# Low parts of differences and of the last weights on GpSimd, one tile's splits issued later, and a product cut in two around the mixing products

## The chip, the core and the metric

The kernel runs on one core of one Trainium2 chip. Its engines are TensorE (PE, with PEld for its weight loads), VectorE (DVE), ScalarE (ACT), GpSimd (POOL) and SyncE (SP), which issues most of the transfers. The metric is the device time of one execution in microseconds; the time before is the median of three runs.

## The reference, cut to what matters

An attention over a narrow local window with a few global columns (8 heads of 64, 768 positions, batch 2), then two blocks. All inputs are 32-bit floats.

```python
def _moe_ref(x, U, V, w_ch1, w_ch2):            # x: 2 x 768 x 512
    xt = x.transpose(0, 2, 1)
    h = xt @ U @ V                              # mixing over positions, rank 32
    u = x + h.transpose(0, 2, 1)
    ch = np.maximum(u @ w_ch1, 0.0) @ w_ch2     # 512 -> 2048 -> 512
    return u + ch

def _moe2_ref(x, mu_k, mu_r, w_k, w_v, w_r):
    x_prev = np.concatenate([np.zeros((B, 1, D), dtype=np.float32), x[:, :-1, :]], axis=1)
    xk = mu_k * x + (1.0 - mu_k) * x_prev
    xr = mu_r * x + (1.0 - mu_r) * x_prev
    k = np.maximum(xk @ w_k, 0.0)               # 512 -> 1024
    v = k * k @ w_v                             # 1024 -> 512
    r = 1.0 / (1.0 + np.exp(-(xr @ w_r)))
    return r * v
```

## The kernel before, in words

**Split numbers.** Each matrix is held as two parts: a high part (a rounded copy, made by ScalarE) and a low part (what the copy left out, a subtraction). A product of two such matrices is three matmuls (`PASS`): high x high, high x low, low x high. The subtraction of a low part has both operands in SBUF and can run on DVE or on POOL. The weights arrive as 64-bit floats and are converted (`conv_steps`): `cvt` (L655, DVE), `c1` (L660, ACT), `c2` (L664, DVE), `c3` (L668, DVE), `high` (L672, ACT), `low` (L676, POOL unless told DVE). A weight is queued with `queue_weight` on a list `bgq`, and `bg` takes one entry of 128 x 512 from it: its load through SP into one of three buffers `stg`, and its steps.

**Stages.** The state is `yp`, 512 rows of features in four blocks of 128 by 2 x 769 columns. It is worked on in three column chunks of 512 (`chunk`: c = 0 lies in batch 0, c = 1 half in each, c = 2 in batch 1). First come the attention and, woven into it, the first block's mixing for batch 0 and the first channel product; the order of each engine there is written out by a planner of the kernel itself (`Flow`, with costs by kind of step). After that the code emits steps in an order made by `weave`, which merges lists evenly, and the framework's scheduler may start a later step before an earlier one whose inputs or buffers are not ready.

**The part after the planner.** The mixing for batch 1 (`u_steps(1)`): transposes, `gms`, `gs`, and then for each feature block the product `hps` (L856) and its addition to `yp` (L861), first for 256 columns, then for 512. `u_split` makes the high and low part of the result for the channel products (L899, L901). Channel products: `ch1` (L926, 512 -> 512 of the 2048 columns, results by L930 and L934) and `ch2` (L948, four of them for each chunk and quarter, one for each output block, each of 12 matmuls into one bank of PSUM, emptied by the addition L952). PSUM banks are of two kinds, `a` and `t`, four of each; `hps` and the products of L948 (`bps`) take `t`.

**The pair product.** For the last three quarters of the 2048 columns, chunks 1 and 2 are multiplied together (`st_pair`) with seven products of half size (L1019) in place of eight. For that `diff_raw` computes differences of the chunks (L972) into `raws`, a tile of the pool of `slot_b`, and `diff_split` calls `parts`, which makes their high (L991) and low part (L992), three for each of two row tiles k. `diff_late` does the same for the fourth (L996, L997). The sums of weights that the pair product needs are made in L730 to L733 and split in L739 and L740.

**The end.** The weights wr, wk and wv of the second block are queued during the last quarter. `st_mix` makes xr and xk (L1204 to L1208), `m_r` is L1241, `m_k` L1221 with its low part on POOL (L1231), `m_out` L1256, L1259 and the store.

Of the kernel before, what the change touches and what calls it, by code (L numbers as in the profile page):

```python
# [7 lines left out]
F32 = mybir.dt.float32  # L8
# [201 lines left out]
def body(tc, out, q, k, v, lim, UV, w1, w2, mu_kr, wk, wv, wr):  # L210
    nc = tc.nc
    with ExitStack() as ctx:
# [403 lines left out]
        def path(general):  # L616
            if general:
                attention_general()
            with ExitStack() as pctx, ExitStack() as fence:
# [6 lines left out]
                def bank(tag, nm):  # L626
                    return pp_.tile([128, 512], F32, tag=tag, name=nm, bufs=banks[tag])
# [69 lines left out]
                def queue_weight(name, src, kt, n, sl):  # L697
                    view = [s.rearrange("p (l k n) -> p l k n", l=2, n=n) for s in sl]
                    per = kt // len(sl)
                    wt[name] = (view, per)  # L700
                    for c0 in range(0, n, 512):
                        for kk in range(kt):
                            hi = view[kk // per][:, 0, kk % per, c0:c0 + 512]
                            lo = view[kk // per][:, 1, kk % per, c0:c0 + 512]
                            s = src[kk * 128:(kk + 1) * 128, c0:c0 + 512]
                            steps = conv_steps((128, 512), hi, lo)
                            if name in ("wr", "wk", "wv") and kk % 2:
                                steps[-1] = ("lo", lambda z, f=steps[-1][1]: f(z, "DVE"))
                            bgq.append((lambda d, s=s: nc.sync.dma_start(out=d, in_=s), steps))

                def wsl(name, l, kk, c0, n):
                    view, per = wt[name]
                    return view[kk // per][:, l, kk % per, c0:c0 + n]
# [193 lines left out]
                def chunk(buf, kk, c, shift=0):  # L907
                    if c == 0:
                        return [(0, 512, buf[:, kk, 1 - shift:513 - shift])]
                    if c == 2:  # L910
                        return [(0, 512, buf[:, kk, 1026 - shift:1538 - shift])]
                    return [(0, 256, buf[:, kk, 513 - shift:769 - shift]),
                            (256, 512, buf[:, kk, 770 - shift:1026 - shift])]
# [23 lines left out]
                def m_ch1(g, c, f, mk=None):  # L937
                    ch1_mm(g, c, f, mk)
                    ch1_high(g, c, f)
                    ch1_low(g, c, f)  # L940

                def m_ch2(g, c, o):
                    r = rs[g, c]
                    ps = bank("t", "bps")
                    n = 0
                    for f in range(4):
                        for lw, lx in PASS:
                            nc.tensor.matmul(ps, lhsT=wsl(("w2", g), lw, f, o * 128, 128), rhs=r[:, lx, f, :],  # L948
                                             start=(n == 0), stop=(n == 11))
                            n += 1  # L950
                    for a, e, ys in chunk(yp, o, c):
                        nc.vector.tensor_tensor(out=ys, in0=ps[:, a:e], in1=ys, op=ALU.add)  # L952

                diffs, sums = [], {}

# [28 lines left out]
                def diff_split(k):  # L984
                    return [lambda x=x, t=t: parts(diffs[0], x, k, raws[4 * k + t]) for x, t in enumerate((0, 1, 3))]
# [3 lines left out]
                def parts(d, x, k, raw):  # L989
                    h, o = d[:, 0, x, k, :], d[:, 1, x, k, :]  # L990
                    nc.scalar.copy(out=h, in_=raw)  # L991
                    nc.vector.tensor_tensor(out=o, in0=raw, in1=h.bitcast(F32), op=ALU.subtract)  # L992

                def diff_late(k):
                    h, o = us[2][:, 0, k, :], us[2][:, 1, k, :]
# [73 lines left out]
                def weave(*streams):  # L1069
                    items = []  # L1070
                    for n, s in enumerate(streams):
                        items += [((x + 0.5) / len(s), n, x, f) for x, f in enumerate(s)]
                    for *_, f in sorted(items, key=lambda v: v[:3]):
                        f()

                def st_ch1(g, c, mk):
                    return [lambda f=f: m_ch1(g, c, f, mk) for f in range(4)]

                def st_ch2(g, c):
                    return [lambda o=o: m_ch2(g, c, o) for o in range(4)]  # L1080
# [4 lines left out]
                def st_bg(n):  # L1085
                    return [lambda: bg(1)] * n
# [93 lines left out]
                    u_split(1, kk, slot_d, 0)  # L1180
                weave(u1[6:8], c0[:1])
                weave(c0[1:3])
                for kk in range(4):
                    u1[8 + kk]()
                    u_split(1, kk, slot_d, 1)
                weave(c0[3:])
                weave(u1[12:])
                actx.close()
                open_slots("sc")
# [77 lines left out]
                def st_diff(*ks_):  # L1267
                    return [f for k in ks_ for f in diff_raw(k)]

                diff_tiles()  # L1270
                weave(st_ch1(0, 1, slot_c), [lambda kk=kk: u_split(2, kk, slot_d) for kk in range(4)] + st_diff(0))
                weave(st_ch1(0, 2, slot_c), st_diff(1) + diff_split(0) + diff_split(1))
                late_ = [lambda k=k: diff_late(k) for k in range(2)]
                if G0 == 1:
                    queue_pair(1)
                else:
                    queue_g(1, slot_a, None)
                weave(st_ch2(0, 1), late_ + st_bg(2))
                queue_g(1, None, slot_c)
                weave(st_ch2(0, 2), st_bg(2))  # L1280
                for g in range(1, NG):
# [53 lines left out]
```

## Time and profile before

| | |
|---|---|
| time, median of 3 runs | 511.78 us (511.73 to 514.96) |
| the profiled execution: time / span | 512.37 us / 510.6 us |
| PE busy / DVE / ACT / POOL | 495.5 / 351.3 / 248.4 / 166.8 us |
| granted TensorE clock | 0.999 |
| moved by DMA, over the span | 91 GB/s from and to HBM |

The profile is one execution. The span is the time from its first to its last instruction; the execution's time as measured from outside is 1.77 us longer. A busy PE is not PE at its peak: matmuls overlap, and the end of each is modelled. An idle time of an engine is put down to what ended last before it.

### The profile page before, as it was taken

To read this page: it belongs to the slowest core of one execution; us is meant where nothing else is said; L and a number is where in the kernel's file an instruction comes from. 1 tells how busy PE (TensorE), PEld (TensorE's weight loads), DVE (VectorE), ACT (ScalarE), POOL (GpSimd) and SP (SyncE) were. 2 spreads that over 40 slices of the span, in tenths; PEclk is the share of its full clock that TensorE was granted. 3 is DMA by queue.
4 is the path that set the end of the run, shared out by engine and by line. 5 is a ranking of instruction groups with operands and counts; after the bars stand their busy time and mean duration, and the time that the engine had idled before them with its cause. 6 is when DMAs were issued, how large, how long until landed. Compare 5 with 4: busy or idle time off the path is not lost.

```text
span 510.6 us, 8677 instructions
## 1 busy us (share of the span) xinstructions
PE 495.5 (97%) x3278; PEld 403.5 (79%) x3278; DVE 351.3 (69%) x756; ACT 248.4 (49%) x566; POOL 166.8 (33%) x217
## 2 busy tenths in 40 slices
PE   7899999999999999999999999999999999999995
PEld 4677688778877888888888887888888888888885
DVE  7899988999998879558794599999055057301211
ACT  6999986554432533025330275736883167013400
POOL 7767685020560534005440033122530034002400
PEclk9999999999999999999999999999999999999999
DMA  8888733310334023300242025333001000100011
GB/s 325 295 310 293 238 113 121 122 42 1 124 101 148 0 83 120 127 1 13 81 155 83 0 64 155 113 107 99 0 21 42 21 1 0 56 28 1 0 44 46
DMA packets 13586, 47.18 MB, mean 92 GB/s; under 512 B 1760, under 2 KB 2144, under 8 KB 13536
## 3 DMA queue, kind: packets, MB, share of 16 engines
q1 hardware_dynamic: 13248, 46.28, 27.0%
q8 instruction: 28, 0.46, 0.4%
q10 hardware_dynamic: 288, 0.26, 0.2%
q14 instruction: 22, 0.18, 0.1%
HBM read 43.39 MB, written 3.15 MB: 91 GB/s over the span
## 4 chain that ended last, share of the span: by engine, by line
PE 72%; DVE 20%; DMA 2%; ACT 2%; issue 2%; POOL 1%; ACTq 0%; DVEq 0%; POOLq 0%; SPq 0%
PE bps L948 19%; PE pvs L1256 13%; PE kps L1221 13%; PE pps L1019 9%; PE aps L926 6%; PE prs L1241 6%; DVE cvc L664 3%; DVE P L471 2%; DVE cvc L668 2%; PE tp L498 2%; PE s L463 2%; DMA stg<-in_w_dram 2%; DVE rs L934 1%; DVE sums L972 1%; DVE yp L952 1%
## 5 line engine op out<-in xcount | busy, mean ns | idle before, releaser
L948 PE MATMUL bps<-rs,w2s 128*128 128x512 f32 x576 | 132.4, 390 | 1.2 <-DVE rs L934 0.6
L948 PEld LDWEIGHTS bps<-rs,w2s 128*128 128x128 f32 x576 | 107.8, 188 | 25.2 <-DVE rs L934 1.0
L926 PE MATMUL aps<-us,w1s 128*128 128x512 f32 x288 | 67.9, 391 | 0.0
L1221 PE MATMUL kps<-mix,wk 128*128 128x512 f32 x288 | 65.8, 389 | 0.0
L1231 POOL TENSOR_TENSOR kl<-kf,kh 128x512 fp32r<-128x512 f32 x24 | 31.5, 1313 | 99.5 <-ACT kh L1230 99.5
L1221 PEld LDWEIGHTS kps<-mix,wk 128*128 128x128 f32 x288 | 54.1, 188 | 11.2
L926 PEld LDWEIGHTS aps<-us,w1s 128*128 128x128 f32 x288 | 53.7, 188 | 11.1
L1256 PE MATMUL pvs<-wv,kh 128*128 128x512 f32 (+1 forms) x208 | 60.4, 373 | 0.0
L676 POOL TENSOR_TENSOR w1s<-cvc,w1s 128x512 fp32r<-128x512 f32 x16 | 24.8, 1569 | 89.6 <-DVE sums L1023 52.9
L664 DVE SCALAR_TENSOR_TENSOR cvc<-cvc,cvt 128x512 uint32<-128x512 uint32 (+1 forms) x53 | 51.1, 973 | 1.9 <-ACT cvc L660 0.9
L660 ACT ACTIVATE cvc<-stg 128x512 f32<-128x512 f32 (+1 forms) x53 | 35.1, 674 | 28.9 <-DMA stg<-in_w_dram 13.4
L491 POOL TENSOR_SCALAR P<-P,sm 128x192 f32<-128x192 f32 x96 | 42.1, 462 | 16.3 <-DVE sm L485 6.7
L1256 PEld LDWEIGHTS pvs<-wv,kh 128*128 128x128 f32 x208 | 38.1, 188 | 6.9
L479 ACT ACTIVATE P<-P,nm 128x192 f32<-128x192 f32 x96 | 42.5, 447 | 1.1 <-DVE nm L471 1.0
L1229 DVE SCALAR_TENSOR_TENSOR kf<-kps,kf 128x512 f32<-128x512 f32 x16 | 11.0, 689 | 46.0 <-ACT kf L1225 46.0
L952 DVE TENSOR_TENSOR yp<-bps,yp 128x512 f32<-128x512 f32 (+1 forms) x64 | 33.5, 547 | 8.0 <-PE bps L948 8.0
L1256 PE MATMUL pvs<-wv,kl 128*128 128x512 f32 (+1 forms) x104 | 38.8, 373 | 0.0
L668 DVE SCALAR_TENSOR_TENSOR cvc<-stg,cvc 128x512 uint32<-128x512 uint32 x52 | 37.4, 727 | 0.4
L655 DVE TENSOR_SCALAR cvt<-stg 128x512 uint32<-128x512 uint32 (+1 forms) x53 | 27.3, 519 | 8.8 <-DMA stg<-in_w_dram 7.4
L1023 DVE TENSOR_TENSOR sums<-pps,sums 128x512 f32<-128x512 f32 x30 | 20.6, 689 | 18.4 <-PE pps L1019 17.9
L1241 PE MATMUL prs<-wr,mix 128*128 128x512 f32 x144 | 33.1, 389 | 0.0
L1259 DVE TENSOR_TENSOR sg<-pvs,sg 128x512 f32<-128x512 f32 (+1 forms) x13 | 8.4, 647 | 35.5 <-PE pvs L1256 35.5
(142 smaller groups left out, 796.2 us busy)
## 6 DMA issues: line engine op xcount, KB each, us to landing
stg<-in_w_dram SPq DMA_DIRECT2D x32, 512.0 KB, 4.2
vin<-in_v_dram SPq DMA_DIRECT2D x8, 768.0 KB, 5.8
KK<-in_k_dram SPq DMA_DIRECT2D x7, 768.0 KB, 6.3
stg<-in_wk_dram SPq DMA_DIRECT2D x8, 512.0 KB, 4.0
stg<-in_wv_dram SPq DMA_DIRECT2D x8, 512.0 KB, 3.5
out_dram<-sg SPq DMA_DIRECT2D x11, 256.0 KB, 2.0
QS<-in_q_dram SPq DMA_DIRECT2D x7, 384.0 KB, 6.1
stg<-in_wr_dram SPq DMA_DIRECT2D x4, 512.0 KB, 3.6
```

What stands on the lines that cost most here:

```text
L479: nc.scalar.activation(out=Px, in_=Px, func=ACTF.Exp, scale=-1.0, bias=z["nm"][:, i, x:x + 1], accum_out=z["sm"][:, i, x:x + 1])
L491: engine.tensor_scalar(out=Px, in0=Px, scalar1=z["sm"][:, i, x:x + 1], scalar2=1.0, op0=ALU.mult, op1=ALU.mult)
L660: nc.scalar.activation(out=z["c"].bitcast(F32), in_=parts(z)[1].bitcast(F32), func=ACTF.Copy, scale=2.0 ** -112)
L664: nc.vector.scalar_tensor_tensor(out=z["c"], in0=z["c"], scalar=3, in1=z["t"], op0=ALU.logical_shift_left, op1=ALU.bitwise_or)
L668: nc.vector.scalar_tensor_tensor(out=z["c"] if plain is None else plain, in0=parts(z)[1], scalar=0x80000000, in1=z["c"], op0=ALU.bitwise_a ...
L926: nc.tensor.matmul(rs[g, c, f], lhsT=wsl(("w1", g), lw, kk, f * 128, 128), rhs=us[c][:, lx, kk, :], start=(kk == 0 and n == 0), stop=(kk = ...
L948: nc.tensor.matmul(ps, lhsT=wsl(("w2", g), lw, f, o * 128, 128), rhs=r[:, lx, f, :], start=(n == 0), stop=(n == 11))
L952: nc.vector.tensor_tensor(out=ys, in0=ps[:, a:e], in1=ys, op=ALU.add)
L1019: nc.tensor.matmul(t, lhsT=a(lw, k, j), rhs=b(lx, k), start=(not on and k == 0 and m == 0), stop=(k == 1 and m == 2), skip_group_check=n i ...
L1221: nc.tensor.matmul(ps, lhsT=wsl("wk", lw, kk, f * 128, 128), rhs=xk[:, lx, kk, :], start=(n == 0), stop=(n == 11))
L1241: nc.tensor.matmul(pr, lhsT=xr[:, lx, kk, t * 128:(t + 1) * 128], rhs=wsl("wr", lw, kk, 0, 512), start=(n == 0), stop=(n == 11))
L1256: nc.tensor.matmul(pv, lhsT=ks[c][lx][:, f, t * 128:(t + 1) * 128], rhs=wsl("wv", lw, f, c0, c1 - c0), start=(n == 0), stop=(n == 23))
```

## The change

The ten low parts of wr, wk and wv with odd kk, which ran on DVE, run on POOL like all others. The low parts of the differences (`parts`) run on POOL. `m_ch2` is cut into `ch2_mm` and `ch2_add`, and for the first quarter, chunk 0, output block 3, the matmuls of its row tiles 0 and 1 are emitted ahead of the first four `hps` of batch 1, those of row tiles 2 and 3 behind them. The three splits of the second row tile's differences (`diff_split(1)`) are emitted with the products L948 of chunk 1 and no longer with the products L926 of chunk 2.

```diff
@@ queue_weight
                             steps = conv_steps((128, 512), hi, lo)
-                            if name in ("wr", "wk", "wv") and kk % 2:
-                                steps[-1] = ("lo", lambda z, f=steps[-1][1]: f(z, "DVE"))
                             bgq.append((lambda d, s=s: nc.sync.dma_start(out=d, in_=s), steps))
@@ m_ch2
+                bs = {}
+
+                def ch2_mm(g, c, o, fs=range(4)):
+                    r = rs[g, c]
+                    if 0 in fs:
+                        bs[g, c, o] = bank("t", "bps")
+                    for f in fs:
+                        for n, (lw, lx) in enumerate(PASS):
+                            nc.tensor.matmul(bs[g, c, o], lhsT=wsl(("w2", g), lw, f, o * 128, 128), rhs=r[:, lx, f, :],
+                                             start=(f == 0 and n == 0), stop=(f == 3 and n == 2))
+
+                def ch2_add(g, c, o):
+                    for a, e, ys in chunk(yp, o, c):
+                        nc.vector.tensor_tensor(out=ys, in0=bs[g, c, o][:, a:e], in1=ys, op=ALU.add)
+
                 def m_ch2(g, c, o):
-                    (the same matmuls and addition in one)
+                    ch2_mm(g, c, o)
+                    ch2_add(g, c, o)
@@ parts
                     nc.scalar.copy(out=h, in_=raw)
-                    nc.vector.tensor_tensor(out=o, in0=raw, in1=h.bitcast(F32), op=ALU.subtract)
+                    nc.gpsimd.tensor_tensor(out=o, in0=raw, in1=h.bitcast(F32), op=ALU.subtract)
@@ path
                 weave(u1[6:8], c0[:1])
                 weave(c0[1:3])
+                ch2_mm(0, 0, 3, (0, 1))
                 for kk in range(4):
                     u1[8 + kk]()
                     u_split(1, kk, slot_d, 1)
-                weave(c0[3:])
+                ch2_mm(0, 0, 3, (2, 3))
+                ch2_add(0, 0, 3)
                 weave(u1[12:])
...
                 weave(st_ch1(0, 1, slot_c), [lambda kk=kk: u_split(2, kk, slot_d) for kk in range(4)] + st_diff(0))
-                weave(st_ch1(0, 2, slot_c), st_diff(1) + diff_split(0) + diff_split(1))
+                weave(st_ch1(0, 2, slot_c), st_diff(1) + diff_split(0))
...
-                weave(st_ch2(0, 1), late_ + st_bg(2))
+                weave(st_ch2(0, 1), late_ + diff_split(1) + st_bg(2))
```

## Rows read from the trace of the kernel before

**Rows 1.** The page's first part: busy us, share of the span, instructions.

```profile
PE 495.5 (97%) x3278; PEld 403.5 (79%) x3278; DVE 351.3 (69%) x756; ACT 248.4 (49%) x566; POOL 166.8 (33%) x217
```

**Rows 2.** Busy time by stretch (us from:to): length, engines, clock, DMA.

```profile
93.65:165.00 71.35, 69.51 (x304) 56.69 (x304) 68.68 (x118) 29.45 (x55) 18.81 (x12) 1.00 0.28 89
...
294.00:311.00 17.00, 16.39 (x72) 13.22 (x72) 16.72 (x27) 11.98 (x21) 7.27 (x4) 1.00 0.31 97
```

**Rows 3.** Timeline of PE: start, us, line, output<-inputs, xcount [idle before <-releaser].

```profile
103.53 0.38 PE L856 MATMUL hps<-uv 96*128 96x256 f32 x1 [1.03 <-DVE yp L952]
...
129.43 16.48 PE L948 MATMUL bps<-rs,w2s 128*128 128x512 f32 x72
146.47 5.71 PE L948 MATMUL bps<-rs,w2s 128*128 128x512 f32 x24 [0.56 <-DVE yp L952]
...
163.31 1.66 PE L1019 MATMUL pps<-diff,w1s 128*128 128x512 f32 x6 [0.25 <-DVE sums L1023]
...
310.70 30.67 PE L948 MATMUL bps<-rs,w2s 128*128 128x512 f32 x134 [0.61 <-DVE rs L934]
```

**Rows 4.** The chain of waits in order of time: start us, us, what.

```profile
99.86 0.68 DVE uv L843
...
154.62 0.60 DVE yp L952
...
182.66 32.64 PE bps L948 x144
...
310.04 0.61 DVE rs L934
...
374.00 21.76 PE pvs L1256 x96
```

**Rows 5.** Groups by line and shape, DVE, whole span: busy us, mean ns | idle.

```profile
L676 DVE TENSOR_TENSOR wk<-cvc,wk 128x512 fp32r<-128x512 f32 x4 | 3.2, 799 | 0.0
...
L676 DVE TENSOR_TENSOR wv<-cvc,wv 128x512 fp32r<-128x512 f32 x4 | 2.7, 685 | 0.7 <-ACT wv L672 0.7
...
L676 DVE TENSOR_TENSOR wr<-cvc,wr 128x512 fp32r<-128x512 f32 x2 | 1.9, 970 | 0.0
```

**Rows 6.** The same groups on DVE between 129 and 150 us.

```profile
L664 DVE SCALAR_TENSOR_TENSOR cvc<-cvc,cvt 128x512 uint32<-128x512 uint32 x6 | 7.3, 1234 | 0.3 <-ACT cvc L660 0.3
L668 DVE SCALAR_TENSOR_TENSOR cvc<-stg,cvc 128x512 uint32<-128x512 uint32 x4 | 3.6, 893 | 0.0
L997 DVE TENSOR_TENSOR us<-sums,us 128x512 fp32r<-128x512 f32 x2 | 3.0, 1482 | 0.0
...
L655 DVE TENSOR_SCALAR cvt<-stg 128x512 uint32<-128x512 uint32 x4 | 2.7, 687 | 0.0
```

**Rows 7.** The same groups on DVE between 294 and 311 us.

```profile
L668 DVE SCALAR_TENSOR_TENSOR cvc<-stg,cvc 128x512 uint32<-128x512 uint32 x4 | 3.5, 870 | 0.0
```

**Rows 8.** Timeline of POOL and of DVE from 300 to 305 us.

```profile
302.39 1.29 POOL L676 TENSOR_TENSOR wk<-cvc,wk 128x512 fp32r<-128x512 f32 x1 [3.17 <-ACT wk L672]
...
300.98 0.68 DVE L668 SCALAR_TENSOR_TENSOR cvc<-stg,cvc 128x512 uint32<-128x512 uint32 x1
...
302.78 1.45 DVE L668 SCALAR_TENSOR_TENSOR cvc<-stg,cvc 128x512 uint32<-128x512 uint32 x1
...
304.75 0.41 DVE L655 TENSOR_SCALAR cvt<-stg 128x512 uint32<-128x512 uint32 x1
```

**Rows 9.** Busy time by stretch again: length, PE, PEld, DVE, ACT, POOL, clock, DMA.

```profile
116.02:128.95 12.93, 12.93 (x58) 10.70 (x58) 12.93 (x27) 6.28 (x12) 0.00 (x0) 1.00 0.01 1
128.99:149.40 20.41, 19.85 (x88) 16.16 (x87) 20.14 (x30) 8.80 (x16) 14.08 (x9) 1.00 0.34 109
```

**Rows 10.** Timeline of DVE and of PE, three places.

```profile
101.18 0.42 DVE L730 TENSOR_TENSOR raw<-cvc 128x256 f32<-128x256 f32 x1
...
153.38 2.88 PE L1019 MATMUL pps<-diff,w1x 128*128 128x512 f32 x12
...
357.23 0.69 DVE L676 TENSOR_TENSOR wv<-cvc,wv 128x512 fp32r<-128x512 f32 x1 [0.69 <-ACT wv L672]
```

More of the change, by code (lines that the diff above doesn't have):

```diff
@@ L940, in m_ch1 @@
                     ch1_low(g, c, f)
-                def m_ch2(g, c, o):
[L943 to L952, printed above, removed]
+                bs = {}
[10 more added lines that the diff above has]
+                        nc.vector.tensor_tensor(out=ys, in0=bs[g, c, o][:, a:e], in1=ys, op=ALU.add)
+                def m_ch2(g, c, o):
+                    ch2_mm(g, c, o)
+                    ch2_add(g, c, o)
                 diffs, sums = [], {}
```

## The prediction

> **What bounds the kernel now.** I read the page's busy line first [rows 1]: TensorE (PE) has work on it for 97% of the span, so at most 15.1 us of the 510.6 are open at all, and VectorE (DVE) at 69% can matter only in places. The table of stretches says where [rows 2]. Up to 93.65 us the order of every engine is written by the planner `Flow`, whose steps and costs the change does not touch. Between 93.65 and 165 us PE is busy for 69.51 of 71.35 while DVE is busy for 68.68, and between 294 and 311 us for 16.39 of 17.00 beside a DVE at 16.72. So the two stretches after the planner in which PE loses anything are those in which DVE is full.
>
> The timeline of PE names the losses one by one [rows 3]. There are four: 1.03 us at 103.53 (the fourth mixing product `hps` waits until DVE's L952 has emptied a PSUM bank), 0.56 us at 146.47 (L948 waits for L952 in the same way), 0.25 us at 163.31 (L1023) and 0.61 us at 310.70 (the last channel result of L934). Together 2.45 us. Matmuls follow each other at 32.64/144 = 0.227 us [rows 4], and 72 of them from 129.43 end at 145.75 [rows 3], which makes the second gap 0.72 instead of 0.56; with 0.16 for each gap the four are 3.1 us. That is a ceiling: nothing in this change takes matmuls away.
>
> The chain of waits [rows 4] shows the same from the other side. From 99.86 us it runs through DVE, instruction after instruction, to the L952 at 154.62 (a full tile of 512 columns counts 0.60 us there, its pitch); from 163 to 294 it is PE; from 294 to 310 it is DVE again, ending in L934; then PE, through the 96 products L1256 from 374.00, to the end.
>
> **Part 1, low parts of wr, wk, wv (10 instructions) from DVE to GpSimd (POOL).** On DVE they are 2 x 0.970 + 4 x 0.799 + 4 x 0.685 = 7.9 us [rows 5]. On POOL one takes between 1.29 us [rows 8] and 14.08/9 = 1.56 us [rows 9], so 13 to 16 us. Most of it lies where PE never waits. What counts are the two for wr and the first for wk, which stand in DVE's queue ahead of the L934 at 310.04: 2 x 0.970 + 0.799 = 2.7 us busy, about 2.5 us at the pitch of the chain.
>
> Against this stands what a POOL instruction costs DVE. One place shows it bare [rows 8]: POOL's low starts at 302.39 and ends at 303.68; DVE's L668, begun at 302.78, needs 1.45 us, where the one at 300.98 took 0.68. Operations whose operands both lie in SBUF are stretched; those that read PSUM (L952, L934) are not. Between 129 and 150 us the means of four such lines [rows 6] lie above the 0.68 us of a full tile (0.41 for L655, as at 304.75 [rows 8]) by 6 x (1.234 - 0.68) + 4 x (0.893 - 0.68) + 2 x (1.482 - 0.68) + 4 x (0.687 - 0.41) = 6.9 us, beside nine POOL instructions [rows 9]: 0.76 us each. Between 294 and 311 us it is 4 x (0.870 - 0.68) [rows 7] + 2 x (0.970 - 0.68) + 4 x (0.799 - 0.68) [rows 5] = 1.8 us beside four [rows 2]: 0.45 us each. The bounds of one are 0 (it falls beside PSUM readers) and 1.3 (DVE waits for all of it). The Trainium skill, page "SBUF — State Buffer", section "Who interferes with whom", says that a DVE instruction with two SBUF inputs and a GpSimd instruction that reads SBUF exclude each other for the whole instruction; rows 8 agree (the wait ends with POOL's instruction). By that rule alone each moved low would cost up to the whole 1.3 us; the rows give 0.45 to 0.76 because part of each falls beside PSUM readers.
>
> So three more POOL lows cost DVE 1.35 to 2.3 us against the 2.5 saved: the last L934 comes 0.2 to 1.15 us earlier (bounds: 2.5 earlier to 1.4 later). The gap there is 0.61 us. I take 0.5 us gained.
>
> Deadlines of the later lows: DVE's last one for wv runs at 357.23 [rows 10], L1256 starts at 374.00 [rows 4]; with one POOL instruction of 1.6 us in its place 15 us are left. All eight lows for wv are 10 to 12.5 us of POOL's time, spread over the loads, so PE's earlier products hide them; without that cover each would cost PE up to 1.6 us.
>
> **Part 2, low parts of the six differences (L992) from DVE to POOL.** DVE loses 6 x 0.60 = 3.6 us at the pitch of a full tile [rows 4]. POOL gets 6 x 1.29 to 1.56 = 7.7 to 9.4 us. It is empty from 116.02 to 128.95, 12.93 us [rows 9], so there is room. The lock costs 6 x 0.45 to 0.76 = 2.7 to 4.6 us (bounds 0 to 7.8): DVE's balance is -0.9 to +1.0 us. DVE's work there is mostly the subtractions L972, with two SBUF inputs, so I do not take the lower price: balance 0. The first reader of the differences starts at 153.38 [rows 10], over 20 us after POOL could be through, so a low that takes twice as long reaches PE nowhere.
>
> **Part 3, the second row tile's splits issued later.** Three copies on ScalarE and three lows move behind the products of L926 into the stretch of L948 from 129.43. No DMA is issued by them, nothing is added. If they really run there, they meet POOL's nine lows of 128.99 to 149.40, busy for 14.08 of 20.41 us [rows 9]; 14.1 + 3 x 1.3 = 18 us still fits before 153.38, at a dearer lock price (0.76 instead of 0.45: 0.9 us for the three). They may not move: the conversion at 101.18 (L730) is written after all of L926 and runs before it [rows 10], so the scheduler takes what is ready. I cost it at nothing, bounds 0 and 0.9; the tile that is held longer (`raws`) is next written by the pair products, whose first reader of a difference starts at 153.38 [rows 10].
>
> **Part 4, the fourth product of L948 cut in two around the mixing products.** The same 12 matmuls and one addition. Six of them (6 x 0.227 = 1.36 us) now stand ahead of the four `hps`, six behind. PE then reaches the fourth `hps` 1.36 us later, at which time the L952 it waited for is done: the 1.03 us are covered. But the product keeps its PSUM bank over the `hps`, and of four banks of that kind only three are left, so the fourth `hps` now waits for the addition L861 of the first. DVE, in order, does that just after the same L952; a half tile takes it 0.42 us [rows 10]. The six remaining matmuls need no bank and can fill that. Bounds: 0 to 1.03 us gained at this place.
>
> **The sum for 93.65 to 165 us.** Three gaps, 1.84 us. What PE gains early it keeps only if DVE, which carries the chain from 99.86 to 155, is earlier as well when L952 is due at 146; with a balance of 0 in part 2 most of the 1.03 us would come back there as waiting. On the other side PE's 0.56 us hang on the order of a few instructions. I take 0.5 us of 1.84. With 0.5 us from the second stretch: 1.0 us. Span 510.6 - 1.0 = 509.6; the profiled run's 512.37 lies 1.77 above its span, so 511.37; the median shown, 511.78, is 0.59 below that run: **510.8 us**.
>
> **Rivals.**
> *The waits only move* (511.8 us). DVE's balance is zero in both stretches, the scheduler orders as before, and each gap closed is opened at the next PSUM bank. For it: the chain through DVE, and L730's place [rows 10]. Against it: the saving in the second stretch is larger than the price by either row.
> *POOL's lock makes DVE later* (slower). Place: L972 and L664 between 116 and 150 us, then L664 and L668 before 310. It decides from a price of 0.60 us for a POOL low in the first stretch and 0.83 in the second (2.5/3). At 0.95, halfway between the 0.60 and the whole 1.3, the first is 6 x 0.95 - 3.6 = 2.1 us later and the second 3 x 0.95 - 2.5 = 0.35: 2.5 us, 514.3 us; with the whole 1.3 it is 4.2 + 1.4 = 5.6 us, 517.4. The skill's rule of part 1 points this way. For it: 0.76 between 129 and 150; against it: the 0.45, and that DVE's conversions can be put off.
> *The bank of part 4* (512.5 us): the fourth `hps` waits for L861 with PE idle; 1.36 us put ahead, less the 1.03 us that this covers, and 0.42 us of waiting make the additions that feed L926 0.75 us later, and nothing later gives it back. Only if the six matmuls behind are not used as filling.
>
> **How the numbers follow.** Forecast 0.50 (its own range 509.3 to 511.4: 0.4 to 2.5 us gained); waits only move 0.25; lock 0.17; bank 0.08. The range 509.2 to 513.8 starts near the ceiling (511.8 - 3.1 = 508.7 cannot be passed by more than noise) and takes in all but the dear half of the lock. A measurement of this kernel can tell about 1%, 5.1 us, from no change. Faster by that would need more than the ceiling: 0.01. Slower by it needs nearly the full lock price: 0.04. Within it: 0.95.
>
> **What would show each step.** No L676 and no L992 on DVE, twenty weight lows on POOL. L934's last before L948's second half near 309 and no idle before that matmul. The four `hps` without the 1.03 us, or with a new wait named L861. L952 near 146 at the same time or earlier. Wrong would be: mean durations of L972 above 1 us (then the lock rival), a PE idle of over 1 us anywhere between 108 and 165, or any at all after 311 us.

## The result and the profile after

The changed kernel takes 519.66 us (median of four runs, 518.99 to 520.85) against 512.08 us for the kernel before on the same chip (511.73 to 514.96): ratio 1.0138, 95% interval 1.0096 to 1.018. By that ratio it is 7 us slower, where 1 us faster was forecast. Line numbers of the changed kernel: L932 is the low channel result (L934 before), L928 its high part (L930 before), L948 the products as before, L953 the addition (L952), L1024 the pair products (L1019), L977 and L997 the differences and their low parts (L972, L992), L1002 the low parts of the fourth differences (L997 before).

The profiled executions differ by 517.4 - 510.6 = 6.8 us of span. Five marks on PE's timeline divide it; the second of them is the six pair products that start at 294.47 (294.04 before). First the changed kernel (start us, us, instructions, what ended the idle time before):

```profile
94.25 3.02 PE L948 MATMUL bps<-rs,w2s 128*128 128x512 f32 x12
...
144.31 8.84 PE L948 MATMUL bps<-rs,w2s 128*128 128x512 f32 x36 [1.69 <-DVE yp L953]
...
294.47 1.52 PE L1024 MATMUL pps<-us,w1s 128*128 128x512 f32 x6
...
308.09 1.52 PE L948 MATMUL bps<-rs,w2s 128*128 128x512 f32 x6
310.10 0.51 PE L948 MATMUL bps<-rs,w2s 128*128 128x512 f32 x1 [0.49 <-ACT rs L928]
312.37 1.34 PE L948 MATMUL bps<-rs,w2s 128*128 128x512 f32 x3 [1.77 <-DVE rs L932]
315.93 32.38 PE L948 MATMUL bps<-rs,w2s 128*128 128x512 f32 x134 [2.22 <-DVE rs L932]
...
348.15 2.20 PE L1248 MATMUL prs<-wr,mix 128*128 128x512 f32 x9
```

Then the kernel before, as far as [rows 3] does not have it:

```profile
93.65 3.74 PE L948 MATMUL bps<-rs,w2s 128*128 128x512 f32 x15
...
294.04 1.52 PE L1019 MATMUL pps<-us,w1s 128*128 128x512 f32 x6
...
307.66 2.43 PE L948 MATMUL bps<-rs,w2s 128*128 128x512 f32 x10
...
341.20 9.00 PE L1241 MATMUL prs<-wr,mix 128*128 128x512 f32 x39
```

| stretch | before | after | difference |
|---|---|---|---|
| to the first L948 | 93.65 | 94.25 | +0.60 |
| from there to the pair products at 294 | 200.39 | 200.22 | -0.17 |
| from there to the 134 matmuls | 16.66 | 21.46 | +4.80 |
| these 134 to the first `prs` | 30.50 | 32.22 | +1.72 |
| `prs` to `pvs` (at 373.84 and 380.79) | 32.64 | 32.64 | 0 |
| `pvs` to the end of the span | 136.76 | 136.61 | -0.15 |

All of the loss that the change explains, 6.5 us, is made at one place. Between 308 and 316 us PE does 10 matmuls and for the rest waits for the channel results. Then the same 134 matmuls take 32.38 us instead of 30.67 [rows 3]. The table of stretches says why (length, then busy us of PE, PEld, DVE, ACT, POOL, then the granted clock):

```profile
305.00:310.00 5.00, 4.61 (x21) 3.48 (x19) 4.79 (x6) 2.18 (x5) 2.52 (x3) 1.00 0.62 209
310.00:315.00 5.00, 1.84 (x4) 0.77 (x4) 4.86 (x7) 2.29 (x5) 2.51 (x2) 0.78 0.59 204
315.00:320.00 5.00, 4.07 (x10) 3.22 (x11) 5.00 (x8) 2.67 (x5) 2.38 (x2) 0.54 0.39 118
```

PE is busy for 1.84 of the 5 us from 310 to 315 and its clock falls. In the next 5 us it has work for most of the time at a granted clock of 0.54, that is nearly all at the lower level of 1.2 GHz. DVE is full throughout. Its timeline there, POOL's four lines first:

```profile
295.42 6.51 POOL L676 TENSOR_TENSOR wr<-cvc,wr 128x512 fp32r<-128x512 f32 x4 [32.43 <-DVE sums L1028]
304.42 2.73 POOL L676 TENSOR_TENSOR wk<-cvc,wk 128x512 fp32r<-128x512 f32 x2 [2.49 <-ACT wk L672]
309.63 1.53 POOL L676 TENSOR_TENSOR wk<-cvc,wk 128x512 fp32r<-128x512 f32 x1 [2.48 <-ACT wk L672]
312.44 1.35 POOL L676 TENSOR_TENSOR wk<-cvc,wk 128x512 fp32r<-128x512 f32 x1 [1.28 <-ACT wk L672]
...
296.37 2.60 DVE L1032 SCALAR_TENSOR_TENSOR rs<-sums,rs 128x512 fp32r<-128x512 f32 x2 [0.29 <-ACT rs L1031]
...
300.10 2.38 DVE L664 SCALAR_TENSOR_TENSOR cvc<-cvc,cvt 128x512 uint32<-128x512 uint32 x2
...
304.81 1.19 DVE L655 TENSOR_SCALAR cvt<-stg 128x512 uint32<-128x512 uint32 x1
306.10 1.59 DVE L664 SCALAR_TENSOR_TENSOR cvc<-cvc,cvt 128x512 uint32<-128x512 uint32 x1
...
310.06 1.65 DVE L668 SCALAR_TENSOR_TENSOR cvc<-stg,cvc 128x512 uint32<-128x512 uint32 x1
...
312.75 1.58 DVE L664 SCALAR_TENSOR_TENSOR cvc<-cvc,cvt 128x512 uint32<-128x512 uint32 x1
...
315.19 0.68 DVE L932 SCALAR_TENSOR_TENSOR rs<-aps,rs 128x512 fp32r<-128x512 f32 x1
```

Eight POOL lows stand there, ahead of the last L932, where four stood before [rows 2], and beside or right behind each group a DVE operation is too long. At 0.68 us for one full tile, 1.28 for two and 0.41 for L655, the excess is 1.32 + 1.10 + 0.78 + 0.91 + 0.97 + 0.90 = 6.0 us, 0.75 us a low. The last L932 starts 20.72 us after the pair products at 294 began, where the last L934 of before started 309.97 - 294.04 = 15.93 us after it: 4.8 us, which is what PE lost before the 134 matmuls.

### The profile page after: what moved, and what is told of

Same layout as the page of the kernel before. It is cut to its first block, busy times and chain, and to the rows that moved or that the text cites. A ratio compares the mean times of both kernels' runs of the same rounds, so it can differ in the third digit from the quotient of the medians.

```text
span 517.4 us, 8687 instructions
## 1 busy us (share of the span) xinstructions
PE 498.0 (96%) x3278; PEld 405.0 (78%) x3278; DVE 353.5 (68%) x740; ACT 249.1 (48%) x566; POOL 189.6 (37%) x233
## 4 chain that ended last, share of the span: by engine, by line
PE 75%; DVE 18%; issue 2%; DMA 2%; ACT 1%; POOL 1%; ACTq 0%; DVEq 0%; POOLq 0%
PE bps L948 21%; PE pvs L1263 13%; PE kps L1228 13%; PE pps L1024 11%; PE aps L924 6%; PE prs L1248 6%; DVE P L471 3%; DVE cvc L664 3%; DVE cvc L668 2%; PE tp L498 2%; DVE sums L977 2%; PE s L463 2%; DVE rs L932 1%; DVE cvt L655 1%; DMA KK<-in_k_dram 1%
## 5 line engine op out<-in xcount | busy, mean ns | idle before, releaser
L948 PE MATMUL bps<-rs,w2s 128*128 128x512 f32 x576 | 135.4, 395 | 6.3 <-DVE rs L932 4.0
L948 PEld LDWEIGHTS bps<-rs,w2s 128*128 128x128 f32 x576 | 108.9, 190 | 31.8 <-DVE rs L932 4.8
L664 DVE SCALAR_TENSOR_TENSOR cvc<-cvc,cvt 128x512 uint32<-128x512 uint32 (+1 forms) x53 | 51.4, 982 | 2.9 <-ACT cvc L660 1.9
L676 POOL TENSOR_TENSOR w1s<-cvc,w1s 128x512 fp32r<-128x512 f32 x16 | 24.6, 1558 | 75.4 <-DVE sums L1028 53.5
L668 DVE SCALAR_TENSOR_TENSOR cvc<-stg,cvc 128x512 uint32<-128x512 uint32 x52 | 41.3, 807 | 0.4
L953 DVE TENSOR_TENSOR yp<-bps,yp 128x512 f32<-128x512 f32 (+1 forms) x64 | 33.6, 548 | 8.0 <-PE bps L948 8.0
L655 DVE TENSOR_SCALAR cvt<-stg 128x512 uint32<-128x512 uint32 (+1 forms) x53 | 32.0, 608 | 7.8 <-DMA stg<-in_w_dram 7.1
L1212 DVE SCALAR_TENSOR_TENSOR mixf<-yp,mu,mixt 128x512 f32<-128x512 f32 (+1 forms) x32 | 19.3, 631 | 22.0 <-ACT mixt L1211 22.0
```

What stands on the lines that cost most here:

```text
L655: nc.vector.tensor_scalar(out=z["t"], in0=parts(z)[0], scalar1=2.0 ** -29, scalar2=7.0, op0=ALU.mult, op1=ALU.min)
L664: nc.vector.scalar_tensor_tensor(out=z["c"], in0=z["c"], scalar=3, in1=z["t"], op0=ALU.logical_shift_left, op1=ALU.bitwise_or)
L668: nc.vector.scalar_tensor_tensor(out=z["c"] if plain is None else plain, in0=parts(z)[1], scalar=0x80000000, in1=z["c"], op0=ALU.bitwise_a ...
L948: nc.tensor.matmul(bs[g, c, o], lhsT=wsl(("w2", g), lw, f, o * 128, 128), rhs=r[:, lx, f, :], start=(f == 0 and n == 0), stop=(f == 3 and ...
```

## The experiments

The theory after this look: POOL's lows, which read SBUF, hold DVE up (the lock), and all of the loss is in part 1. Rivals: the order of DVE's conversions changed (more of them stand ahead of the last L932), part 2 costs as well, or the lows of wv hold PE up later.

**Which part.** Part 1 alone on the kernel before:

```diff
-                            if name in ("wr", "wk", "wv") and kk % 2:
-                                steps[-1] = ("lo", lambda z, f=steps[-1][1]: f(z, "DVE"))
```

> The kernel before with part 1 alone: the ten odd low parts of wr, wk, wv on POOL, nothing else. Theory A (all of the loss sits in part 1: POOL's reads hold up DVE's conversions ahead of the last L934 of the last quarter): 518 to 520 us, PE idle of 4 to 6 us between 308 and 317 us, and a granted clock under 0.9 just behind it. Theory B (parts 2 to 4 share in the loss, through the later start of the pair product): 513 to 516 us.

519.48 us, ratio 1.0124 (1.0103 to 1.0146). PE waits at the same three places as in the changed kernel, 0.47, 1.78 and 2.51 us, and the 134 matmuls are as slow:

```profile
315.62 32.80 PE L946 MATMUL bps<-rs,w2s 128*128 128x512 f32 x134 [2.51 <-DVE rs L932]
```

The opposite, the changed kernel with those two lines put back (parts 2 to 4 stay):

> The changed kernel with part 1 undone: the ten odd lows on DVE again, parts 2 to 4 kept. Theory A: 511 to 512.3 us, the wait at 310 us as before (0.6 us), the mixing products without their wait of 1.03 us. Theory B: 514 us or more.

513.01 us, ratio 1.0013 (0.9998 to 1.0028), 0.7 us above theory A's range and 1 us below B's. The wait at 310 is 0.61 us again, as in [rows 3], and the 134 matmuls take 30.67 us. So part 1 makes the loss, and the other three together make none that stands clear of the noise. The 1.03 us of the fourth `hps` [rows 3] is gone in this kernel, and a wait of 1.68 us for an addition at 144.72 stands in its place and in that of the 0.56.

**Why: reads on POOL, or order on DVE.** The kernel before, with the even lows of wr, wk and wv computed twice on POOL; every instruction of DVE keeps its place:

```diff
+                            elif name in ("wr", "wk", "wv"):
+                                steps[-1] = ("lo", lambda z, f=steps[-1][1]: (f(z), f(z)))
```

> The kernel before, but each of the ten even low parts of wr, wk, wv is computed twice on POOL, the same result written again; DVE keeps its ten odd lows and its order is that of the kernel before. Theory lock: four more POOL reads ahead of the last L934 at 310 us, each 0.5 to 1.0 us on DVE: the idle of PE at 310.70 grows from 0.6 to 2.5 to 4.5 us, and the time to 514 to 518 us. Theory order: PE's wait stays at 0.6 and the time at 511.5 to 512.5 us.

520.61 us, ratio 1.0153 (1.0131 to 1.0175). That is above the 514 to 518 us expected. Nothing was taken from DVE and nothing moved in its order, and the loss is there with the same face on PE's timeline (DVE's behind it):

```profile
310.72 0.73 PE L950 MATMUL bps<-rs,w2s 128*128 128x512 f32 x2 [1.25 <-DVE rs L936]
...
315.61 32.36 PE L950 MATMUL bps<-rs,w2s 128*128 128x512 f32 x134 [3.28 <-DVE rs L936]
...
296.82 3.49 DVE L1029 SCALAR_TENSOR_TENSOR rs<-sums,rs 128x512 fp32r<-128x512 f32 x2
...
312.60 1.75 DVE L668 SCALAR_TENSOR_TENSOR cvc<-stg,cvc 128x512 uint32<-128x512 uint32 x1
...
314.88 0.68 DVE L936 SCALAR_TENSOR_TENSOR rs<-aps,rs 128x512 fp32r<-128x512 f32 x1
```

The last L936 starts 314.88 - 294.09 = 20.79 us after the pair products, 4.9 us later than in the kernel before. Again eight POOL lows stand ahead of it in place of four, so each of the four added cost 1.2 us, of the 1.5 us that one takes there (3.01 us for two at 310.79). The granted clock is 0.74 from 310 to 315 us and 0.58 in the 5 us behind.

The converse keeps the changed kernel's order on DVE and takes POOL's reads away: all 20 lows of wr, wk and wv become a memset on POOL (the low parts of these weights are left out of the computation):

```diff
+                            if name in ("wr", "wk", "wv"):
+                                steps[-1] = ("lo", lambda z, o=lo: nc.gpsimd.memset(o.bitcast(F32), 0.0))
```

> The changed kernel, but all twenty low parts of wr, wk, wv are one memset to zero on POOL (the low parts are left out; PE's work is the same). The order of DVE's instructions is exactly that of the changed kernel, and between 294 and 340 us POOL no longer reads SBUF at all. It differs from the run with only the odd lows replaced in that the even lows are gone too and POOL's writes are a third as many. Theory lock (the stretched conversions come from POOL's reads, whichever low it is): L664 and L668 between 299 and 316 us at 0.67 to 0.75 us each, PE idle there under 1.2 us, time 511.3 to 513.3 us. Theory order (conversions in front of the last channel results cost that even at full speed): PE idle of 3 us or more, time 515.5 us or more.

513.07 us, ratio 1.0005 (0.9991 to 1.0018). The DVE operations that took 2.38 and 1.19 us take 1.29 and 0.42, and of PE's waits one of 1.07 us is left:

```profile
299.87 1.29 DVE L664 SCALAR_TENSOR_TENSOR cvc<-cvc,cvt 128x512 uint32<-128x512 uint32 x2
...
303.49 0.42 DVE L655 TENSOR_SCALAR cvt<-stg 128x512 uint32<-128x512 uint32 x1
...
312.47 30.67 PE L950 MATMUL bps<-rs,w2s 128*128 128x512 f32 x134 [1.07 <-DVE rs L934]
```

The order alone therefore costs 1.07 - 0.61 = 0.46 us at this place; the rest comes from POOL's lows. These two runs decide between the theories: the order theory falls.

A run in between did not separate them. Only the ten odd lows were replaced, each by three memsets, so that POOL stays busy but reads nothing for them (their low parts are left out); the even lows still read:

```diff
+                            if name in ("wr", "wk", "wv") and kk % 2:
+                                steps[-1] = ("lo", lambda z, o=lo: [nc.gpsimd.memset(o.bitcast(F32), 0.0) for _ in range(3)])
```

> The changed kernel, but POOL fills the ten odd low parts of wr, wk, wv with zeros (three memsets each) in place of the subtraction: the low parts are left out, the PE work is the same, and the instructions of DVE stand in exactly the order of the changed kernel. POOL then only writes. Theory lock (POOL's reads of SBUF stretch DVE's two-input operations): L664 and L668 between 300 and 316 us fall from means above 1 us toward 0.7 to 0.9, the PE idle there falls from 4.5 us to under 1.5, time 511.5 to 514 us. Theory order (the scheduler has put more conversions ahead of L934): PE idle and time stay, 517 us or more.

518.1 us, ratio 1.0108 (1.0083 to 1.0132): the lock theory had asked for much less. Its timeline shows what was overlooked, the even lows, and one thing more:

```profile
299.24 1.81 POOL L676 TENSOR_TENSOR wr<-cvc,wr 128x512 fp32r<-128x512 f32 x1
300.99 3.45 POOL L708 MEMSET wk<- 128x512 f32 x7
...
309.90 2.39 POOL L708 MEMSET wv<- 128x512 f32 x5
...
299.22 2.38 DVE L664 SCALAR_TENSOR_TENSOR cvc<-cvc,cvt 128x512 uint32<-128x512 uint32 x2
...
302.13 1.28 DVE L668 SCALAR_TENSOR_TENSOR cvc<-stg,cvc 128x512 uint32<-128x512 uint32 x2
...
311.03 1.53 DVE L655 TENSOR_SCALAR cvt<-stg 128x512 uint32<-128x512 uint32 x1
```

L664 at 299.22 is stretched by a low that was left reading. The two L668 at 302.13, with two inputs in SBUF, run at full speed beside memsets: it is POOL's reading that holds up such an operation, and not that POOL is busy. L655, one input and a scalar, 0.41 us when alone, takes 1.53 us beside memsets. The Trainium skill, page "SBUF — State Buffer", section "Who interferes with whom", makes the same distinction: two SBUF inputs contend with a GpSimd instruction that reads and not with one that only writes, while an operation like `tensor_scalar` can enter a mode that takes the shared pair for itself. The rows agree with both halves. Since the even lows' reads and many writes remained, the time of this run tells the theories apart in no way.

**Which of the ten lows.** Three kernels, each the changed one with some odd lows back on DVE:

```diff
+                            if name == "wk" and kk % 2:
+                                steps[-1] = ("lo", lambda z, f=steps[-1][1]: f(z, "DVE"))
```

With those of wk back, as here:

> The changed kernel with the four odd lows of wk on DVE again, those of wr and wv on POOL. If the price comes per POOL low ahead of the last L934 (six with both wr lows moved, against eight in the changed kernel and four or five in the kernel before): 513.5 to 517 us, PE idle of 1.5 to 3.5 us around 311 us. If wk's lows alone carry the loss: 511.5 to 512.5 us. If wr's alone: 517.5 us or more.

518.68 us, ratio 1.0117 (1.009 to 1.0144). That is the time expected if wr's lows alone made the loss, but the next run shows that those of wk cost as well. With `name == "wr"` in the condition, so that those of wr are back:

> The changed kernel with the two odd low parts of wr back on VectorE; those of wk and wv stay on GpSimd. The lock theory: between 294 and 316 us GpSimd has six reading instructions in place of eight, and the two that go are the pair of 6.5 us that stood at 295; VectorE's work before the last channel result is about 2 us earlier at the 0.7 us per low measured so far, less the 2 x 0.97 us that it computes itself, so by the prices alone nothing is won: 517 to 520 us, with TensorE waiting 4 us or more for the channel results. The rival, that only the first two lows (those of wr) matter because they start the delay of everything that is queued behind: 512 to 515 us, with waits of TensorE there below 1.5 us in all and the clock at its full level through 310 to 320.

517.21 us, ratio 1.0077 (1.0058 to 1.0096); PE waits 1.69 us for ACT and 1.54 for DVE, less than the 4 us expected, and the 134 matmuls begin at the lower clock. With both names, so that only wv's lows stay on POOL:

> The changed kernel with the odd low parts of wr and wk back on VectorE; only the four of wv stay on GpSimd. If the loss sits before the last channel results (lock theory with its place at 294 to 316 us): as with all ten on VectorE, 512 to 513.5 us, and TensorE waits 0.6 us near 311. If the lows of wv also hold TensorE up, behind GpSimd's own work for the key products: a wait of TensorE for a low part of wv or of the keys between 345 and 385 us, and 514 to 517 us.

513.12 us, ratio 1.0012 (0.9999 to 1.0025), the time of the kernel with all ten back, with the wait of 0.61 us at 311.65 as the only one after 165 us. So wv's lows are hidden, and the loss is made by those of wr and wk. They do not add up: with wk back the 134 matmuls begin 314.33 - 294.77 = 19.56 us after the pair products at 294 begin, with wr back (133 of them) 19.81, against 16.66 before and 21.46 with both on POOL; and in each case they begin at the lower clock. PE with wr back:

```profile
312.32 0.74 PE L950 MATMUL bps<-rs,w2s 128*128 128x512 f32 x2 [1.69 <-ACT rs L930]
314.60 1.65 PE L950 MATMUL bps<-rs,w2s 128*128 128x512 f32 x3 [1.54 <-DVE rs L934]
```

Three matmuls in 1.65 us (with wk back four in 1.89) are the pace of the lower clock.

**Parts 2 and 4 by themselves.** Part 2 alone on the kernel before:

```diff
-                    nc.vector.tensor_tensor(out=o, in0=raw, in1=h.bitcast(F32), op=ALU.subtract)
+                    nc.gpsimd.tensor_tensor(out=o, in0=raw, in1=h.bitcast(F32), op=ALU.subtract)
```

> The kernel before with only the low parts of the six differences moved to GpSimd. The lock theory with the price of 0.45 to 0.76 us per low: VectorE's balance between 116 and 150 us is -0.9 to +1.0 us, and the waits of TensorE for the additions at 146 move by as much: 511.5 to 513.5 us. A price as in the stretch of the last weights with all of the six in full (1.3 us each) would give 4.2 us more: 516 to 517 us.

515.1 us, ratio 1.0044 (1.003 to 1.0059), between the two cases expected. In its trace the wait for an addition at 146 is 2.03 us instead of 0.56, and from the first L948 to the pair products at 294 PE takes 1.36 us longer than in the kernel before. Part 4 alone:

```diff
+                ch2_mm(0, 0, 3, (0, 1))
                 for kk in range(4):
                     u1[8 + kk]()
                     u_split(1, kk, slot_d, 1)
-                weave(c0[3:])
+                ch2_mm(0, 0, 3, (2, 3))
+                ch2_add(0, 0, 3)
```

> The kernel before with only the product cut in two around the mixing products. If waits only move: the wait of about 1 us of the fourth mixing product is gone, and TensorE waits about 1.5 us for an addition near 145 us in place of 0.6; the time is that of the kernel before, 511.5 to 513 us. If the gap is truly won: 510.5 to 511.5 us. If the bank held over the mixing products costs: a new wait of TensorE near 105 us behind the half-tile additions of the mixing, 512.5 to 513.5 us.

512.97 us, ratio 1.0 (0.9988 to 1.0011). The 1.03 us shrink to 0.32 and 0.17, the second of them for L861, the wait that the bank rival named; the wait at 146 is gone too, but at 163.75 stands one of 0.92 where 0.25 stood:

```profile
106.02 0.39 PE L856 MATMUL hps<-uv 96*128 96x256 f32 x1 [0.17 <-DVE yp L861]
163.75 1.66 PE L1026 MATMUL pps<-diff,w1s 128*128 128x512 f32 x6 [0.92 <-DVE sums L1030]
```

The wait moved, by 17 us further than expected. Part 2 alone loses about 2 us, part 4 alone gains nothing, and the two with part 3 come out at the time of before. So parts 3 and 4 together take up most of what part 2 loses. Part 3 was not run alone, nor either of them with part 2 only, so which of them does it is not shown.

**Ways out.** If the lows hold up the channel results, the conversions of wk could be held back until these are done. The changed kernel with five wk conversions queued to start after the last L932:

```diff
-                weave(st_ch2(3, 0), st_bg(4))
-                weave(st_ch2(3, 1), st_bg(3), st_mix(0, 1, slot_b))
+                weave(st_ch2(3, 0), st_bg(2) + st_bg_after(2, lambda: marks[3, 0, 3]))
+                weave(st_ch2(3, 1), st_bg_after(3, lambda: marks[3, 0, 3]), st_mix(0, 1, slot_b))
```

(`marks` holds the L932 instructions; `st_bg_after` issues a conversion step behind the one given.)

> The changed kernel with all lows on POOL, and DVE's conversions of wk queued behind the last channel result of L932 in the last quarter (issue order only, nothing computed otherwise). Theory lock in front of L932: it does not matter how dear a conversion is if none stands ahead of L932, so the PE idle around 310 us falls under 0.5 us, the granted clock stays at 1.0 there, time 511 to 512.7 us. If POOL's load itself were the cause (low parts of wr or wk late for PE): 515 us or more, with PE waiting for POOL at L1248 or L1228.

516.75 us, ratio 1.0071 (1.0053 to 1.0089). The place is healed and the loss comes back behind it (PE's timeline, then one stretch of 5.5 us from the table):

```profile
307.95 32.80 PE L948 MATMUL bps<-rs,w2s 128*128 128x512 f32 x144
...
368.54 10.10 PE L1234 MATMUL kps<-mix,wk 128*128 128x512 f32 x36 [1.85 <-ACT kf L1238]
```

```profile
368.50:374.00 5.50, 5.46 (x17) 4.33 (x18) 0.00 (x0) 5.29 (x10) 4.27 (x4) 0.69 0.00 0
```

All 144 matmuls run at 0.228 us without a gap, and `prs` starts at 340.59, earlier than in the kernel before (341.20). But the conversions of wv, which follow those put off, now run on ACT among its evictions of the products `prs` and `kps`; PE waits for these (0.74 us at 358.21 for one of `prs`, 1.85 for one of `kps`), and the clock falls there. So the time is 4 us above the 511 to 512.7 expected. A two-fold fence on the kernel with part 1 undone (wk as above, and the conversions of the second quarter of w2, at 146, behind the last addition of the second row half):

> The changed kernel with part 1 undone (odd lows on DVE), the wk conversions queued behind the last L934 as in the run above, and the w2 conversions of the second quarter queued behind the last addition of L955 for chunk 1. If the two remaining PE waits (1.7 us at 144 for a PSUM bank, 0.6 us at 311 for L934) are made by conversions standing ahead of them on DVE, both go: 2.3 us less than the run with part 1 undone, 510 to 511 us. If they only move on: 512.5 to 513.5 us.

514.52 us, ratio 1.0025 (1.0009 to 1.004): the waits at 146 and at 310 are gone, and one of 2.45 us stands at 163.80, followed by 5 us at a clock of 0.66. The time lies above both cases expected. DVE is the bound between 94 and 165 us, and putting work off there only moves the wait.

A gentler form on the kernel before: the cut product of part 4, and the wk conversions behind the second and the fourth channel result, with every low on the engine it was on:

```diff
+                weave(st_ch2(3, 0), st_bg(2) + st_bg_after(2, lambda: marks[3, 0, 1]))
+                weave(st_ch2(3, 1), st_bg_after(3, lambda: marks[3, 0, 3]), st_mix(0, 1, slot_b))
```

> The kernel before with the cut product, and with five of the wk conversions queued so that they start after the second and the fourth channel result of the last group rather than before them; no low part changes its engine. If the 0.6 us wait for the last channel result near 310 us closes and nothing else opens: 0.6 us less than the cut product alone, 511 to 512.5 us. If waits only move: TensorE waits for the key products or for the last weights between 345 and 385 us instead, and the time is that of the cut product alone or up to 2 us more.

511.36 us, ratio 0.9975 (0.9964 to 0.9986), the lowest ratio of this study: a quarter of a per cent, 1.3 us by the ratio, and the interval lies below 1. Two waits of PE are left after 93 us, 1.00 us at 163.34 and the one below, and the 144 matmuls run without a gap:

```profile
307.70 32.83 PE L950 MATMUL bps<-rs,w2s 128*128 128x512 f32 x144
378.52 0.50 PE L1271 MATMUL pvs<-wv,kl 128*128 128x512 f32 x1 [0.36 <-POOL kl L1246]
```

## Why the prediction was wrong, point by point

**What bounds the kernel.** Right: the two stretches in which DVE is full are those where the time is decided, and PE's end follows DVE's L934 in the second.

**Part 1.** This is the step that failed: "three more POOL lows cost DVE 1.35 to 2.3 us against the 2.5 saved: the last L934 comes 0.2 to 1.15 us earlier". It came 4.8 us later. Four terms were off.
1. *The saving.* Two lows at 0.970 and one at 0.799 [rows 5] were counted with the stretch that other POOL lows had put on them. Taken off DVE, they leave 3 x 0.60 = 1.8 us; the stretch stays and falls on the next operation.
2. *The price and its count.* The price was charged for three new lows alone, at 0.45 to 0.76 us. In the event all eight lows of the stretch cost 0.75 on average, the old ones too: 6.0 us, where the kernel before had (1.27 - 0.67) + (1.45 - 0.68) = 1.4 us ahead of its last L934 (the first low of wr at 295.58, and the L668 of [rows 8]). That is 4.6 us more, against 1.8 saved. The lows added are four, as the delay lets a further one of wk in ahead of the last L932: 1.15 us each, and 1.2 in the run that computes the even lows twice. The price of 0.45 was an average over four lows, of which those at 297.51 and 308.04 cost DVE nothing ahead of its last L934; it was no property of a low.
3. *What comes with the delay.* As L932 gets later, one more L668 and one more L655 are ready and stand ahead of it, 0.60 + 0.35 = 0.95 us, and DVE has 0.64 us of gaps of its own (0.29 + 0.10 + 0.11 + 0.04 + 0.10). 4.6 - 1.8 + 0.95 + 0.64 = 4.4 of the 4.8 us; the rest I have not split further, each gap also loses the overlap of 0.08 us that two neighbouring operations have.
4. *The clock.* No step had it: 32.38 - 30.67 = 1.7 us.

So the upper bound of the sum ("1.4 later") was passed by a factor of more than four (4.8 + 1.7). The later lows, those of wv, were hidden, as forecast: the run with wv alone shows it.

**Part 2.** The price was too kind here as well. In the changed kernel L977's excess over unstretched operations (0.68 us, 0.41 for the narrow ones) is 4.7 us beside seven POOL lows between 116 and 130, 0.67 each. The two L655 at 127.33, beside the last two of the seven, took 2.36 us where two unstretched ones take 0.75: with them it is 6.3 us, 0.90 each, above the 0.45 to 0.76 forecast and near the 0.95 of the lock rival. L977's groups by shape between 108 and 133 us, busy us and mean ns, and the L655:

```profile
L977 DVE TENSOR_TENSOR sums<-yp 128x256 f32<-128x256 f32 x4 | 2.7, 689 | 0.0
L977 DVE TENSOR_TENSOR sums<-yp,sums 128x512 f32<-128x512 f32 x2 | 2.7, 1339 | 0.0
L977 DVE TENSOR_TENSOR sums<-yp,sums 128x256 f32<-128x256 f32 x4 | 2.6, 690 | 0.0
L977 DVE TENSOR_TENSOR sums<-yp 128x512 f32<-128x512 f32 x2 | 2.5, 1228 | 0.0
...
127.33 2.36 DVE L655 TENSOR_SCALAR cvt<-stg 128x512 uint32<-128x512 uint32 x2
```

At 0.90 the balance is 6 x 0.90 - 3.6 = 1.8 us lost, where 0 was taken; alone part 2 costs 2.2 us of time (ratio 1.0044), 1.36 of them up to the pair products at 294. In company with parts 3 and 4 the loss is gone, but the 0.5 us that the sum had gained for this stretch do not show either (ratio 1.0013, interval 0.9998 to 1.0028).

**Part 3.** No run shows a cost of its own. The splits did not move into the stretch of L948, as the forecast allowed: all six lows L997 start between 116.75 and 127.93, before the first L948 of chunk 1 at 128.86, and in the run of part 2 alone, without part 3, between 118.8 and 130.4. What moved are the two lows of the fourth differences, which part 3 does not name: they stand at 135.16 and take 1.28 us together, where the kernel before had 1.18 and 1.78 for them ([rows 6] has the mean).

**Part 4.** The 1.03 us was covered, and the wait for an addition at 144 is 1.69 us against 0.56 [rows 3]. That this is the same microsecond come back is not shown, for part 2 alone makes a wait of 2.03 us there, and part 4 alone has its new wait at 163.75. The forecast kept 0.5 us of the stretch; the table has 0.17. The rival that waits only move is what happened in this stretch.

**The rivals.** The one that was right got a chance of 0.17: POOL's lock makes DVE later, 514.3 to 517.4 us. Its mechanism is shown by the two runs that double POOL's lows and take them away with DVE's order kept; its time was short by 2 us, as it counted three lows and not the clock. Its place was half right: in the first stretch the stretched operations are there, but the changed kernel as a whole lost nothing. Its deciding point (0.83 us a low in the second stretch) was wrong for the reason of terms 1 and 2: by the true saving and the true count the balance is lost already at (1.8 + 1.4)/8 = 0.40 us a low. With the seven lows that could be counted beforehand it is 0.46, at the lower of the two prices of the rows, and 0.76 gives 7 x 0.76 - 3.2 = 2.1 us lost: a sum built on that would have found nothing to gain there. The signs named under "wrong would be" stand in the trace: L977 above 1 us for full tiles (1.23 and 1.34; 0.69 for the narrow ones), a wait above 1 us before 165, and waits after 311.

The first stretch, to the first L948, is 0.60 us longer in the changed kernel, in which nothing of it was altered. It was between 0.47 and 1.41 us longer in the profiles of most kernels here, and not longer in that with the lows computed twice (93.66) nor in that with two fences (93.69). The kernel before itself varies by more than that between executions (511.58 to 513.85 us in one set of 28). What makes it stays open.

## What to carry to other kernels

Where VectorE and GpSimd both read SBUF, a cheap operation moved from the one to the other may be no relief: here 0.60 us was saved by each, and each GpSimd operation added ahead of the last channel result cost VectorE 1.15 us, as those that were on GpSimd already got dearer with it. Count every GpSimd instruction in the stretch at the dearest price the trace shows, take the saving at the unstretched duration, and ask which wait of TensorE stands behind VectorE's last result. The stall of TensorE counted twice here, 4.8 us as lost time and 1.7 us for the matmuls that followed at the lower clock.

## What the runs showed of the hardware that I had not expected

**GpSimd can be the one that is held up.** In the kernel before, POOL's low at 308.04 took 3.14 us, twice its usual time, while DVE ran L664, L655, L668 and L664 without a break and none of them was stretched:

```profile
308.04 3.14 POOL L676 TENSOR_TENSOR wk<-cvc,wk 128x512 fp32r<-128x512 f32 x1 [4.36 <-ACT wk L672]
...
308.76 0.68 DVE L668 SCALAR_TENSOR_TENSOR cvc<-stg,cvc 128x512 uint32<-128x512 uint32 x1
...
309.97 0.68 DVE L934 SCALAR_TENSOR_TENSOR rs<-aps,rs 128x512 fp32r<-128x512 f32 x1
310.57 1.16 DVE L676 TENSOR_TENSOR wk<-cvc,wk 128x512 fp32r<-128x512 f32 x1
```

The low ends at 311.18, 1.21 us after 309.97, where DVE's reader of PSUM begins, so it seems to get through there; and then DVE's L676 at 310.57 is the one that waits. In [rows 8] the same: the low starts at 302.39, during an L934, and the L668 behind it is stretched. That fits an access to SBUF that stays with the engine whose instructions follow each other, and passes on at a reader of PSUM or a gap; no run was made for this rule alone, and it is not shown. It would explain why the price rose: the more POOL lows, the more gaps on DVE, and every gap lets the next one in.

**The clock.** In the changed kernel, after 308 to 316 us with 10 matmuls on it, PE's next ten took 4.24 us on the chain of waits, 0.42 us each, against 0.227 [rows 4]:

```profile
315.93 4.24 PE bps L948 x10
```

In the run with the fence, without idle time at this place, 144 matmuls kept 0.228. A single wait of 2.03 us (part 2 alone, at 146) left the granted clock at 1.00 in the stretches behind it; one of 2.45 us (two fences, at 163.80) was followed by 5 us at 0.66, and one of 1.85 us (the fence on the changed kernel, at 368.54) by 5.5 us at 0.69. So the length of the wait alone does not tell these cases apart.
